# Score products of two tiles per TensorE run, value products of a batch in one run: attention ahead of a dense layer, fp32, one core

## The chip, the core and the metric

The kernel runs on one core of one Trainium2 chip. The time is the device time of one execution in microseconds (us). Before the change the median of three runs is 931.36 us (931.02 to 931.78); one execution was recorded by the hardware profiler, with a span of 929.1 us at the full granted TensorE clock (1.000).

Engines are named as the profile names them: PE is TensorE's matmul, PEld its weight load, DVE VectorE, ACT ScalarE, POOL GpSimd, SP the engine that issues most transfers. `L258` is line 258 of the kernel before.

## The reference, cut to what matters

All in fp32. Batch 8, 8 heads, 576 tokens, head width 64. Keys and values are averaged over groups of 8 tokens, so 72 keys are left per head.

```python
k_p = k.reshape(B, H, Sp, pool, D).mean(axis=3)          # 576 tokens -> 72 keys
v_p = v.reshape(B, H, Sp, pool, D).mean(axis=3)
scores = scale * np.matmul(q, k_p.transpose(0, 1, 3, 2))
scores = scores - np.max(scores, axis=-1, keepdims=True)
attn = np.exp(scores)
attn = attn / (np.sum(attn, axis=-1, keepdims=True) + 1e-09)
attn_out = np.matmul(attn, v_p)
x = attn_out.transpose(0, 2, 1, 3).reshape(B * S, H * D)  # 4608 x 512
h = x @ w_in                                              # 512 -> 2048
s = np.sin(alpha * h)
g = h + s * s / (alpha + 1e-09)
out = g @ w_out                                           # 2048 -> 512
```

## The kernel before

**Two stages.** Up to about 530 us the kernel computes attention and `g` together: while TensorE does the first dense layer for one block of 512 tokens (`u`, nine of them), the attention of a later batch is woven in. After that comes the second dense layer (L963), which the change does not touch.

**Slots.** The first dense layer uses a fast scheme with seven products in place of eight. A block `u` has 28 slots, four groups `J` of seven (`k` = 0 to 6). Each slot ends with one product: four matmuls of 256 columns, which the profile records as eight (L666). What follows from the product of slot `k` on ScalarE and VectorE (`left0` to `left6`) is issued at the start of the next slot, ahead of the attention work of that slot. Every engine runs its instructions in the order in which they are written here.

```python
def left0(): b6 = bank(); scalar.copy(b6, b1)                 # L692; then squares of the group before (L679)
def left1(): finish(Q)                                        # VectorE, L733: two adds for the group before
def left2(): store_g(Q); b7 = bank(); scalar.copy(b7, b6)     # L704
             scalar.copy(p5, b5)                              # L706
def left3(): sin(b1); square                                  # ScalarE, L672, L679
def left4(): add(g[1,:,1], b7, p5)                            # VectorE, L645
def left5(): add(g[0,:,1], b6, p5); sin(g[1,:,1])             # VectorE L645, ScalarE L672
             add(g[0,:,0], b1, s)                             # VectorE, L645
def left6(): sin(g[0,:,1]); [square]; sin(b7)                 # ScalarE
# ...
p = (1, 5, 6, 2, 7, 3, 4)[k]     # products of the slots; 1 and 5 start b1 and b5,
                                 # 6 adds into b6, 2 into b1, 7 into b7, 3 into b6, 4 into b7
product(p, ...)                  # L666
```

So product 6 waits for the copy L692, product 7 for the copy L704, and product 4 (slot k = 6) for the add of `left4`, which reads b7 first. There are eight PSUM banks of 512 fp32 columns: five turn for the dense layer (four per group), and three (5, 6, 7) serve the attention (`abank`).

**Scores.** A batch has 576 tokens: four tiles of 128 and one of 64 rows. A score tile is 16 matmuls of 64 x 64 (64 x 32 for the last tile), 72 columns each, recorded as 32 (L258); heads of one half (`e`) share a bank.

```python
def products(i):
    ps = [self.abank([P, NP, Sp]) for e in range(2)]
    for hp in range(NP):
        for r, q in columns(hp, i):
            for e in range(2):
                s = slice(64 * e, 64 * e + 64)
                k = kb[s, hp, :] if b else self.kb2[s, 2 * hp + e, :]
                nc.tensor.matmul(ps[e][r:r + q.shape[-1], hp, :], q[s], k, start=True, stop=True)
    return ps
def shift(i, e, ps):
    # n rows: 128, or 64 for the last tile
    nc.vector.tensor_reduce(out=mx[:n], in_=ps[:n], axis=AX, op=OP.max)                      # L265
    nc.vector.tensor_tensor(out=ex[...], in0=ps[:n], in1=mx..., op=OP.subtract)              # L266
def score(i):
    for e, ps in enumerate(products(i)):
        shift(i, e, ps)
def exp(i):    # ScalarE, L275: one activation over the tile's 8 heads x 72
def norm(i):   # VectorE: sum over the keys (L287), reciprocal (L279); GpSimd: product (L280)
def turn(i):   # VectorE: 32 x 32 transposes of ex into tr (L404, L405)
def move(part):
    for a in (2 * part, 2 * part + 1):
        for s in range(2):
            for c in range(2):
                nc.sync.dma_start(out=..., in_=...)      # tr to aM, L416: 16 transfers per batch
```

The tile `tr` is one buffer; `turn_q` (L194) writes it again for the next queries, after the moves have landed.

**Values.** The main run (slot 25) holds 512 tokens of each head pair in four banks; the 64 tokens left follow one slot later in two banks. In both, 64 of the 72 keys come first (64 x 64 tiles) and the last 8 keys after them (32 x 128 tiles).

```python
def values(hps, banks):
    for o, (main, _) in zip(ps, parts):
        for e, (w, x) in enumerate(main):
            nc.tensor.matmul(o[64 * e:64 * e + 64], w, x, start=True, ...)                   # L456
    for o, (_, (w, x)) in zip(ps, parts):
        nc.tensor.matmul(o, w..., x, start=False, stop=True, ...)                            # L458
    for hp, o in zip(hps, ps):
        to_x(...)                                                                            # ScalarE, L431
def values_rest(banks):
    ps = [self.psum([P, 2, 64], i) for i in banks]
    # the same in two steps, L478 and L481, and to_x
```

**The schedule** of attention work by slot, for the first block and for the steady ones:

```python
# u == 0 (batch 1):
    for i in range(5):
        at((4, 5, 6, 7, 8)[i], A.q_t, i)
        at((7, 8, 9, 11, 12)[i], A.score, i)
        at((9, 9, 14, 14, 15)[i], A.exp, i)
        at((10, 10, 15, 15, 16)[i], A.norm, i)
        at((13, 13, 16, 17, 17)[i], A.turn, i)
    at(10, self.combine_w_in, 2, (0, 1, 2, 3), self.nc.gpsimd)
    at(10, self.combine_w_in, 3, (0, 1, 2, 3), self.nc.gpsimd)
    at(17, A.move, 0); at(17, A.move, 1)
    # ...
# 0 < u < last (batches 2 to 7):
    for i in range(5):
        at((1, 3, 4, 5, 6)[i], A.score, i)
        at((8, 9, 10, 10, 10)[i], A.exp, i)
        at((9, 10, 11, 11, 12)[i], A.norm, i)
        at((12, 12, 13, 14, 14)[i], A.turn, i)
    at(14, A.move, 0); at(14, A.move, 1)
    # turn_q in slots 22 to 25
    at(25, lambda: A.values((0, 2, 1, 3), A.free_banks()))
    at(26, lambda: A.values_rest((5, (self.turn + 1) % 5)))
    at(26, self.att[b + 1].k_t)                          # L228: keys of the next batch
```

Of the kernel before, what the change touches and what calls it, by code (L numbers as in the profile page):

```python
# [13 lines left out]
F32 = mybir.dt.float32  # L14
AX = mybir.AxisListType.X
AF = mybir.ActivationFunctionType
OP = mybir.AluOpType
PSUM = bass.MemoryType.PSUM

P = 128  # L20
# [20 lines left out]
class Kernel:  # L41
# [171 lines left out]
    def attention(self, b):  # L213
# [2 lines left out]
        kb, ex = self.kblk[b % 2], self.ex  # L216
        rows = (P, P, P, P, 64)
        scale = 1.0 / (D ** 0.5) / POOL
        row = lambda i: 5 if b == 0 else i
        E = lambda n, i, h0, h1: ex[:n, row(i), h0:h1, 0:Sp]  # L220
        aT = []

        def k_t():
# [18 lines left out]
        def columns(hp, i):  # L242
# [4 lines left out]
                return [(64 * c, self.qt[b][:, i, hp, 2 * c:2 * c + 2].rearrange("p t i -> p (t i)")) for c in range(2)]  # L247
            return [(32 * a, self.qt[b][:, a, hp, 4]) for a in range(2)]

        def products(i):  # L250

            ps = [self.abank([P, NP, Sp]) for e in range(2)]
            for hp in range(NP):
                for r, q in columns(hp, i):
                    for e in range(2):
                        s = slice(64 * e, 64 * e + 64)
                        k = kb[s, hp, :] if b else self.kb2[s, 2 * hp + e, :]
                        nc.tensor.matmul(ps[e][r:r + q.shape[-1], hp, :], q[s], k, start=True, stop=True)  # L258
            return ps

        def shift(i, e, ps):

            n = rows[i]
            mx = self.sm.tile([P, NP], F32, name="mx")
            nc.vector.tensor_reduce(out=mx[:n], in_=ps[:n], axis=AX, op=OP.max)  # L265
            nc.vector.tensor_tensor(out=ex[:n, row(i), e::2, 0:Sp] if b == 0 else ex[:n, i, 4 * e:4 * e + 4, 0:Sp], in0=ps[:n],  # L266
                                    in1=mx[:n].unsqueeze(2).to_broadcast([n, NP, Sp]), op=OP.subtract)

        def score(i):
# [1 line left out]
                shift(i, e, ps)  # L271

        def exp(i):
            e = E(rows[i], i, 0, H)
            nc.scalar.activation(out=e, in_=e, func=AF.Exp, scale=scale)  # L275

        def divide(i, sm, eng):
            n = rows[i]
            nc.vector.reciprocal(out=sm[:n], in_=sm[:n])  # L279
            eng.tensor_tensor(out=E(n, i, 0, H), in0=E(n, i, 0, H),  # L280
                              in1=sm[:n].unsqueeze(2).to_broadcast([n, H, Sp]), op=OP.mult)

        def norm(i):

            n = rows[i]
            sm = self.sm.tile([P, H], F32, name="sm")
            nc.vector.tensor_reduce(out=sm[:n], in_=ex[:n, i, :, 0:Sp + 1], axis=AX, op=OP.add)  # L287
            divide(i, sm, nc.gpsimd)

        def new_a():  # L290
            self.aM = self.ap.tile([P, 4, 5, 5, 32], F32, name="aM")

        def k_head(hp):

# [24 lines left out]
        def products_head(hp):  # L319
# [3 lines left out]
            for e in range(2):  # L323
                for tp in range(2):
                    q = self.qt_tiles(b)[:, hp, 2 * e + tp, :]
                    for r in (0, 64):
                        for u in range(2):
                            s = slice(64 * u, 64 * u + 64)
                            nc.tensor.matmul(ps[r:r + 64, u, 2 * e + tp, :], q[s, r:r + 64], self.kb2[s, 2 * hp + e, :], start=True, stop=True)

        exs = ex[:].rearrange("p i h c -> p (i h) c")

        def soft_head(hp):

# [34 lines left out]

        def a0_views():  # L370

            x = self.aM[:].rearrange("p a h t i -> p (a h t i)")[:, 0:5 * S].rearrange("p (h n) -> p h n", h=5)
            return x[:, 0:4], x[:, 4]

        def a_head(g, banks):
# [20 lines left out]
            nc.scalar.copy(out=self.last_t[:], in_=ps)  # L396

        def turn(i):
            n = rows[i]
            if i == 0:  # L400
                self.tr = self.new_tr()
            tr = self.tr[:n].rearrange("p (c s h t i) -> p c s h t i", c=2, s=2, h=5, i=32)[:, :, :, :, i, :]
            x = ex[:n, i].rearrange("p (s h) k -> p s h k", s=2)
            nc.vector.transpose(out=tr[:, :, :, 0:4].rearrange("p c s h i -> p s h c i"), in_=x[..., 0:64].rearrange("p s h (c i) -> p s h c i", c=2))  # L404
            nc.vector.transpose(out=tr[:, :, :, 4].rearrange("p c s (h k) -> p c s h k", h=4),  # L405
                                in_=x[..., 64:Sp].unsqueeze(1).to_broadcast([n, 2, 2, 4, Sp - 64]))

        def move(part):

            tr = self.tr.rearrange("p (c s h t i) -> p c s h t i", c=2, s=2, h=5, i=32)  # L410
            for a in (2 * part, 2 * part + 1):
                flat = lambda x: x.rearrange("p h t i -> p h (t i)")[:, :, 0:160 if a < 2 else 128]
                for s in range(2):
                    for c in range(2):
                        r = 64 * s + 32 * c
                        nc.sync.dma_start(out=flat(self.aM[r:r + 32, a]), in_=flat(tr[32 * a:32 * a + 32, c, s]))  # L416

        def to_x(ps, hp, t0, m):

# [14 lines left out]
        def value_parts(hp, rest):  # L434

            vm, vz = self.vp[b]
            g, s = divmod(hp, 2) if b == 0 else (hp % 2, hp // 2)
            if b == 0:
                aM, aR = (self.last_t[:, 0:4], self.last_t[:, 4]) if rest else a0_views()
                w = slice(0, 64) if rest else slice(0, 4 * P)  # L440
                r = 32 * hp
                return ([(vm[64 * s:64 * s + 64, 2 * g + e], aM[64 * s:64 * s + 64, 2 * g + e, w]) for e in range(2)],
                        (vz[r:r + 32, 0:2], aR[r:r + 32, w]))
            order = lambda x: x.rearrange("p a t i -> p t a i") if b == 1 else x.rearrange("p a t i -> p a (t i)")
            at = lambda r, n, h: self.aM[r:r + n, 0:2, h, 4, :] if rest else order(self.aM[r:r + n, :, h, 0:4, :])
            r = 64 * s + (0 if rest else 32 * g)
            return ([(vm[64 * s:64 * s + 64, 2 * g + e], at(64 * s, 64, 2 * g + e)) for e in range(2)],
                    (vz[r:r + 32, 2 * g:2 * g + 2], at(r, 32, 4)))

# [9 lines left out]
            for hp, o in zip(hps, ps):  # L459
                to_x(o.rearrange("p (t j) -> p j t", t=4), hp, 0, 512)  # L460

        def free_banks():

            return 5, 6, 7, (self.turn + 4) % 5

        def values_rest(banks):

            order = (0, 1, 2, 3) if b == 0 else (0, 2, 1, 3)
            parts = {hp: value_parts(hp, True) for hp in order}
            if b == 0:  # L470
                ps = [self.psum([P, 64], i) for i in banks]
                at = dict(zip(order, ps))
            else:
                ps = [self.psum([P, 2, 64], i) for i in banks]
                at = {hp: ps[hp // 2][:, hp % 2] for hp in order}
            for j, hp in enumerate(order):
                for e, (w, x) in enumerate(parts[hp][0]):
                    nc.tensor.matmul(at[hp][64 * e:64 * e + 64], w, x, start=(b == 0 or j < 2), stop=False, skip_group_check=True)  # L478
            for hp in order:
                w, x = parts[hp][1]  # L480
                nc.tensor.matmul(at[hp], w.rearrange("p e d -> p (e d)"), x, start=False, stop=True, skip_group_check=True)  # L481
            self.vp.pop(b)
            for i, x in enumerate(ps):
                to_x(x, i if b == 0 else slice(2 * i, 2 * i + 2), 512, 64)

        return SimpleNamespace(**{f.__name__: f for f in (k_t, q_t, products, score, exp, norm, new_a, turn, move, values, values_rest, free_banks,
                                                          k_head, q_head, rest_q, products_head, soft_head, norm_head, norm_rest, a_head, a_rest)})


# [325 lines left out]
    def carry(self, u):  # L815
# [5 lines left out]
        if u == 0:  # L821
# [15 lines left out]
            at(7, self.load_v, 1, 1)  # L837
            for i in range(5):
                at((4, 5, 6, 7, 8)[i], A.q_t, i)
                at((7, 8, 9, 11, 12)[i], A.score, i)  # L840
                at((9, 9, 14, 14, 15)[i], A.exp, i)
                at((10, 10, 15, 15, 16)[i], A.norm, i)
                at((13, 13, 16, 17, 17)[i], A.turn, i)
            at(10, self.combine_w_in, 2, (0, 1, 2, 3), self.nc.gpsimd)
            at(10, self.combine_w_in, 3, (0, 1, 2, 3), self.nc.gpsimd)
            at(15, A0.exp, 4)
            at(20, A0.norm_rest)
            at(23, A0.a_rest)
# [1 line left out]
            at(17, A.new_a)  # L850
            at(17, A.move, 0)
            at(17, A.move, 1)
            at(25, lambda: A.values((0, 2, 1, 3), A.free_banks()))
            at(26, lambda: A.values_rest((5, (self.turn + 1) % 5)))
            at(9, self.load_q, 2)
            at(14, self.load_q, 3)
            for e in range(2):
# [5 lines left out]
            at(0, self.sums_of_x, u, 3)  # L863
        if 0 < u < last:
            A = self.att[b]
            for i in range(5):
                at((1, 3, 4, 5, 6)[i], A.score, i)
                at((8, 9, 10, 10, 10)[i], A.exp, i)
                at((9, 10, 11, 11, 12)[i], A.norm, i)
                at((12, 12, 13, 14, 14)[i], A.turn, i)  # L870
            at(14, A.new_a)
            at(14, A.move, 0)
            at(14, A.move, 1)
            for i in range(2):
                at((0, 1)[i], self.load_v, b, i)
                if b < last:
                    at(12, self.load_k, b + 1, i)
            at(25, lambda: A.values((0, 2, 1, 3), A.free_banks()))
            at(26, lambda: A.values_rest((5, (self.turn + 1) % 5)))
            if b < last:  # L880
                at(26, self.att[b + 1].k_t)
            if u + 3 <= last:
# [324 lines left out]
```

## Time and profile before

| | |
|---|---|
| time | 931.36 us (931.02 to 931.78) |
| span in the profile | 929.1 us |
| granted TensorE clock | 1.000 |
| period of a steady batch (one `u`) | 57.35 us |
| in one such period (151.20 to 208.55): PE, PEld busy | 57.35, 46.50 us |
| DVE, ACT, POOL busy in it | 38.89, 39.60, 19.66 us |
| first block (35.50 to 94.00): PE, DVE, ACT, POOL busy | 55.50, 41.49, 44.21, 35.63 us of 58.50 |

The busy time of PE counts a matmul until its result is out, and matmuls overlap, so PE looks busy also where the starts are further apart than they need be. The starts say more: two L666 records in a row start 0.216 us apart.

An answer of the profile is read like this. In the chain, each row is a start in us, a duration in us, and what ran: engine, tile, line, how often. In the timeline, a bracket at the end of a row gives the idle time of the engine ahead of it and the instruction that ended it.

### The profile page before, as it was taken

The page shows a single profiled execution, that of the slowest core. Times are in us where ns is not written, and L with a number is a line of the kernel's source. Part 1 is how long each engine was busy: PE and PEld are TensorE (multiplying, and loading weights), DVE is VectorE, ACT ScalarE, POOL GpSimd, SP SyncE. Part 2 cuts the span into 40 slices and gives each one's busy share as a digit, 9 for nine tenths or more (in the row PEclk, how much of TensorE's full clock was granted, in tenths as well). Part 3 has the DMA queues.
Part 4 walks back from the last instruction along what each step waited for, and adds up shares of the span by engine and source line. Part 5 has one row for each costly group of instructions (what it writes and reads, how often), then busy time and mean ns, then how long its engine had stood idle before and what let it go on. Part 6 is the DMA issues. An engine that isn't in the chain of part 4 may idle for free.

```text
span 929.1 us, 17658 instructions
## 1 busy us (share of the span) xinstructions
PE 912.3 (98%) x6953; PEld 815.0 (88%) x6953; DVE 687.6 (74%) x1060; ACT 439.8 (47%) x1011; POOL 158.9 (17%) x154
## 2 busy tenths in 40 slices
PE   7999999999999999999999999999999999999997
PEld 6676887878878788787888899999999999999997
DVE  7576776757767576673366889988888888988894
ACT  4686586775857658676786631111111211112111
POOL 4284250522505225050000000000000000000000
PEclk9999999999999999999999999999999999999999
DMA  9975655857567556635626247162536353443501
GB/s 251 241 200 167 183 155 167 241 168 189 158 179 218 172 137 160 181 110 169 256 83 207 91 142 217 40 205 51 175 82 166 90 158 99 138 118 110 147 14 39
DMA packets 141298, 141.12 MB, mean 152 GB/s; under 512 B 49808, under 2 KB 111008, under 8 KB 141216
## 3 DMA queue, kind: packets, MB, share of 16 engines
q1 hardware_dynamic: 140144, 138.81, 51.9%
q10 hardware_dynamic: 1072, 1.19, 0.5%
q8 instruction: 55, 0.90, 0.4%
q14 instruction: 27, 0.22, 0.1%
HBM read 75.37 MB, written 47.19 MB: 132 GB/s over the span
## 4 chain that ended last, share of the span: by engine, by line
PE 93%; ACT 2%; DVE 1%; issue 0%; DMA 0%; POOL 0%; SPq 0%; DVEq 0%; ACTq 0%; POOLq 0%
PE PS L666 45%; PE PS L963 41%; PE PS L258 3%; PE PS L456 2%; PE PS L458 1%; PE PS L481 0%; ACT s L672 0%; PE PS L478 0%; ACT ex L275 0%; PE PS L228 0%; DVE h L733 0%; DVE h L645 0%; ACT s L679 0%; PE PS L239 0%; DMA out_dram<-o 0%
## 5 line engine op out<-in xcount | busy, mean ns | idle before, releaser
L666 PE MATMUL PS<-home,a 128*128 128x256 f32 x1152 | 267.2, 382 | 1.0 <-DVE h L645 1.0
L666 PEld LDWEIGHTS PS<-home,a 128*128 128x128 f32 x1152 | 215.0, 190 | 38.7 <-issue 5.3
L666 PE MATMUL PS<-home,as 128*128 128x256 f32 x864 | 201.1, 382 | 1.2 <-POOL a L537 1.2
L666 PEld LDWEIGHTS PS<-home,as 128*128 128x128 f32 x864 | 161.5, 190 | 25.4 <-POOL a L537 1.6
L963 PE MATMUL PS<-s,wb 128*128 128x144 f32 x896 | 119.3, 286 | 0.4 <-ACT PS L1076 0.4
L963 PEld LDWEIGHTS PS<-s,wb 128*128 128x128 f32 x896 | 113.7, 190 | 0.7 <-ACT PS L1076 0.6
L679 ACT ACTIVATE s<-s,c 128x256 f32<-128x256 f32 (+1 forms) x216 | 110.0, 572 | 0.0
L117 POOL TENSOR_TENSOR kvin<-kvin 96x768 f32<-96x768 f32 (+3 forms) x42 | 69.1, 1646 | 205.3 <-DMA kvin<-in_v_dram 192.5
L645 DVE TENSOR_TENSOR h<-PS,p 128x512 f32<-128x512 f32 x72 | 49.2, 684 | 64.2 <-PE PS L666 33.3
L672 ACT ACTIVATE s<-h,al 128x256 f32<-128x256 f32 x144 | 65.1, 501 | 53.7 <-DVE h L645 53.7
L1076 ACT COPY PS<-PS 128x144 f32<-128x144 f32 x56 | 14.7, 263 | 146.0 <-PE PS L963 144.6
L672 ACT ACTIVATE s<-PS,al 128x256 f32<-128x256 f32 x144 | 60.2, 469 | 37.8 <-DVE h L733 20.1
L963 PE MATMUL PS<-r,wb 128*128 128x144 f32 x512 | 73.2, 286 | 0.0
L963 PE MATMUL PS<-s,a 128*128 128x144 f32 x512 | 73.2, 286 | 0.0
L963 PEld LDWEIGHTS PS<-r,wb 128*128 128x128 f32 x512 | 67.1, 190 | 0.1
L963 PEld LDWEIGHTS PS<-s,a 128*128 128x128 f32 x512 | 67.0, 190 | 0.0
L733 DVE TENSOR_TENSOR h<-PS,s 128x512 f32<-128x512 f32 x36 | 24.7, 685 | 50.8 <-ACT s L679 50.7
L1095 ACT COPY PS<-PS 128x144 f32<-128x144 f32 x56 | 14.7, 263 | 88.2 <-PE PS L963 88.2
L963 PE MATMUL PS<-s,we 128*128 128x144 f32 x384 | 54.9, 286 | 0.0
L963 PE MATMUL PS<-x,wb 128*128 128x144 f32 x384 | 54.9, 286 | 0.0
L963 PEld LDWEIGHTS PS<-s,we 128*128 128x128 f32 x384 | 50.3, 190 | 0.1
L963 PEld LDWEIGHTS PS<-x,wb 128*128 128x128 f32 x384 | 50.3, 190 | 0.0
(170 smaller groups left out, 1208.4 us busy)
## 6 DMA issues: line engine op xcount, KB each, us to landing
g_bridge<-h SPq DMA_DIRECT2D x72, 512.0 KB
r<-g_bridge SPq DMA_DIRECT2D x31, 1152.0 KB
out_dram<-o SPq DMA_DIRECT2D x128, 72.0 KB
kvin<-in_k_dram SPq DMA_DIRECT2D x14, 576.0 KB
q<-in_q_dram SPq DMA_DIRECT2D x7, 1024.0 KB
kvin<-in_v_dram SPq DMA_DIRECT2D x14, 512.0 KB
aM<-tr SPq DMA_DIRECT2D x56, 100.0 KB
aM<-tr SPq DMA_DIRECT2D x56, 80.0 KB
```

The source lines that it names most:

```text
L117: self.nc.gpsimd.tensor_tensor(out=t[..., 0:w] if w > D else out, in0=t[..., 0:w], in1=t[..., w:2 * w], op=OP.add)
L258: nc.tensor.matmul(ps[e][r:r + q.shape[-1], hp, :], q[s], k, start=True, stop=True)
L456: nc.tensor.matmul(o[64 * e:64 * e + 64], w, x, start=True, stop=False, skip_group_check=True)
L458: nc.tensor.matmul(o, w.rearrange("p e d -> p (e d)"), x, start=False, stop=True, skip_group_check=True)
L645: add = lambda o, x, y: nc.vector.tensor_tensor(out=o, in0=x, in1=y, op=OP.add)
L666: nc.tensor.matmul(ps[:, jj, :], self.A[p][:, kk, f * P:(f + 1) * P], x[:, kk, :], start=(start and jj == 0 and kk == 0), stop=(kk == 1), ...
L672: nc.scalar.activation(out=G.s[:, i, jj, j, :], in_=src[:, jj], func=AF.Sin, scale=self.al[:, f:f + 1])
L679: nc.scalar.activation(out=x, in_=x, func=AF.Square, scale=self.c[:, f:f + 1])
L733: add = lambda o, x, y: self.nc.vector.tensor_tensor(out=o, in0=x, in1=y, op=OP.add)
L963: nc.tensor.matmul(out, W[:, J // 2, J % 2, :], A[:, J, :], start=(start and J == 0), stop=(J == self.NJ - 1), skip_group_check=True)
L1076: nc.scalar.copy(out=x1[:, 0, :], in_=x0[:, 1, :])
L1095: nc.scalar.copy(out=x1[:, 1, :], in_=x1[:, 0, :])
```

## The change

Three things are changed in batches 1 to 7; batch 0 keeps its own path.

1. **Scores of two tiles per run.** `two_scores(j)` does the matmuls of tiles `2j` and `2j + 1` in one run, in four banks: 5 and 6 for the first, and for the second bank 7 with the bank of the five that is free at that time. The 64-token tile has no run of its own: its scores go with tile 3, into the free columns of that tile's two banks, as two more head columns (6 in place of 4). Maximum and subtract then take both banks in one instruction, 576 elements a row, or 864 for tile 3. Exponential, sum, reciprocal, product and turn take four tiles in place of five, the last one 12 heads wide. In the second run tile 3 is shifted ahead of tile 2.
2. **Values of all 576 tokens in one run.** `all_values` joins the main products and those of the last 64 tokens, which now share one bank; two copies of one element on VectorE keep products of different row halves in that bank apart. The layout of `aM` and `tr` changes with it: each of the 16 moves is one piece of 736 or 704 elements a row.
3. **Places in the schedule.** Two score runs in slots 3 and 5 (10 and 12 in the first block) in place of five; in the first block exponentials, sums and turns lie in slots 14 to 17, and GpSimd's fourth combination of weights moves from slot 10 to 16.

The purpose is fewer visits of TensorE to its small tiles, each of which costs a change there and back, and fewer instructions on VectorE and ScalarE.

```diff
+        def two_scores(j):
+            x = (self.turn + 1) % 5
+            views = []
+            for i, (c, d) in ((2 * j, (5, 6)), (2 * j + 1, (x, 7))):
+                m = 6 if i == 3 else NP
+                ps = self.PS[:, c:d + 1:d - c, 0:m * Sp].rearrange("p e (h k) -> p e h k", h=m)
+                views.append((i, m, ps))
+                for t in (i, 4) if i == 3 else (i,):
+                    for hp in range(NP):
+                        r0, h = (64 * (hp // 2), NP + hp % 2) if t == 4 else (0, hp)
+                        for r, q in columns(hp, t):
+                            for e in range(2):
+                                s = slice(64 * e, 64 * e + 64)
+                                nc.tensor.matmul(ps[r0 + r:r0 + r + q.shape[-1], e, h, :], q[s], kb[s, hp, :], start=True, stop=True)
+            for i, m, ps in views[::-1 if j else 1]:
+                mx = self.sm.tile([P, 2, 6], F32, name="mx2")
+                nc.vector.tensor_reduce(out=mx[:, :, 0:m], in_=ps, axis=AX, op=OP.max)
+                nc.vector.tensor_tensor(out=E(i).rearrange("p (e h) k -> p e h k", e=2), in0=ps,
+                                        in1=mx[:, :, 0:m].unsqueeze(3).to_broadcast([P, 2, m, Sp]), op=OP.subtract)
 ... (exp, norm: four tiles, tile 3 with 12 heads)
         def turn(i):
+            nc.vector.transpose(out=main..., in_=x[:, :, 0:4, 0:64]...)
+            if i < 3:
+                nc.vector.transpose(out=keys, in_=x[:, :, 0:4, 64:Sp]...)
+            else:
+                for c in range(2):
+                    nc.vector.transpose(out=keys[:, c], in_=x[:, :, 0:4, 64:Sp])
+                nc.vector.transpose(out=tr[..., 640:704]..., in_=x[:, :, 4:6, 0:64]...)
+                for s in range(2):
+                    nc.vector.transpose(out=tr[:, 0, s, 704:736]..., in_=x[:, s, 4:6, 64:Sp]...)
 ... (move: 16 transfers, each 736 or 704 elements a row)
+        def all_values():
+            hps = 0, 2, 1, 3
+            ps = dict(zip(hps, (self.psum([P, 4 * P], i) for i in (5, 6, 7, (self.turn + 4) % 5))))
+            rest = self.psum([P, 4, 64], (self.turn + 1) % 5)
 ...
+            def ordered():
+                nc.vector.tensor_copy(out=self.sm.tile([P, 1], F32, name="order")[:], in_=rest[:, 1, 0:1])
+            halves(ps[2], main[2], True)
+            halves(rest[:, 0], more[0], True)
+            halves(rest[:, 1], more[1], False)
+            ordered()
+            for hp in (0, 1):
+                halves(ps[hp], main[hp], True)
+            halves(rest[:, 2], more[2], False)
+            halves(rest[:, 3], more[3], False)
+            halves(ps[3], main[3], True)
+            for o, hp in ((rest[:, 0], 0), (rest[:, 1], 1)):
+                last_keys(o, more[hp])
+            ordered()
+            for hp in hps:
+                last_keys(ps[hp], main[hp])
+            for hp in (2, 3):
+                last_keys(rest[:, hp], more[hp])
 ... (to_x for the five banks)
 # u == 0
-                at((7, 8, 9, 11, 12)[i], A.score, i)
-                at((9, 9, 14, 14, 15)[i], A.exp, i)
-                at((10, 10, 15, 15, 16)[i], A.norm, i)
-                at((13, 13, 16, 17, 17)[i], A.turn, i)
+            for i in range(2):
+                at((10, 12)[i], A.two_scores, i)
+            for i in range(4):
+                at((14, 15, 15, 15)[i], A.exp, i)
+                at((15, 15, 16, 16)[i], A.norm, i)
+                at((16, 16, 17, 17)[i], A.turn, i)
-            at(10, self.combine_w_in, 3, (0, 1, 2, 3), self.nc.gpsimd)
+            at(16, self.combine_w_in, 3, (0, 1, 2, 3), self.nc.gpsimd)
 # 0 < u < last
-                at((1, 3, 4, 5, 6)[i], A.score, i)
-                at((8, 9, 10, 10, 10)[i], A.exp, i)
-                at((9, 10, 11, 11, 12)[i], A.norm, i)
-                at((12, 12, 13, 14, 14)[i], A.turn, i)
+            for i in range(2):
+                at((3, 5)[i], A.two_scores, i)
+            for i in range(4):
+                at((8, 9, 10, 10)[i], A.exp, i)
+                at((9, 10, 11, 11)[i], A.norm, i)
+                at((12, 12, 13, 13)[i], A.turn, i)
-            at(25, lambda: A.values((0, 2, 1, 3), A.free_banks()))
-            at(26, lambda: A.values_rest((5, (self.turn + 1) % 5)))
+            at(25, A.all_values)
```

## The prediction, made before the changed kernel was run

> **What bounds the kernel now.** I read the page's busy shares first, then the chain that ended last.
>
> ```profile
> PE 912.3 (98%) x6953; PEld 815.0 (88%) x6953; DVE 687.6 (74%) x1060; ACT 439.8 (47%) x1011; POOL 158.9 (17%) x154
> ...
> PE 93%; ACT 2%; DVE 1%; issue 0%; DMA 0%; POOL 0%; SPq 0%; DVEq 0%; ACTq 0%; POOLq 0%
> ```
>
> TensorE is the bound, and only time on its own stream counts. Next comes the chain in order of time for one batch in the steady part (start, duration, what):
>
> ```profile
> 218.07 0.66 PE PS L258 x32
> 218.74 1.92 PE PS L666 x8
> ...
> 225.83 0.64 PE PS L258 x32
> 226.46 33.19 PE PS L666 x152
> 259.65 1.88 PE PS L456 x16
> 261.53 1.07 PE PS L458 x8
> 262.60 1.93 PE PS L666 x8
> 264.53 0.39 PE PS L478 x16
> ```
>
> A slot is eight L666 records. 152 of them take 33.19 us, so a slot alone is 1.73 to 1.75 us; between two score runs it is 1.92. The single starts in the trace say why. L666 starts are 0.216 us apart; the first score starts 0.309 after the last L666; eight groups of four run 0.0625 us apart, the first 0.05 late; then L666 comes back 0.11 late and its second record at 0.320 instead of 0.216. A score run thus holds 0.50 us of work and 0.093 + 0.05 + 0.11 + 0.104 = 0.36 us of switching. The batches repeat every 57.35 us with almost no gap on TensorE.
>
> But the chain in a later batch shows who stands just behind it:
>
> ```profile
> 284.31 8.07 PE PS L666 x37
> 292.38 0.48 ACT PS L704
> 292.87 0.51 ACT p L706
> 293.38 1.74 ACT ex L275 x3
> ...
> 296.13 0.69 DVE h L645
> 296.87 20.99 PE PS L666 x96
> ```
>
> The copy into b7, three exponentials, a row sum and the add of left4 release slot 13 with no time to spare. The timeline of the weight loads shows the same two places one batch earlier, by what ended the idle time in brackets:
>
> ```profile
> 235.07 1.59 PEld L666 LDWEIGHTS PS<-home,a 128*128 128x128 f32 x8 [0.18 <-ACT PS L704]
> ...
> 238.67 3.32 PEld L666 LDWEIGHTS PS<-home,a 128*128 128x128 f32 x16 [0.28 <-DVE h L645]
> ```
>
> So in slots 9 to 13 ScalarE and VectorE have zero slack, although their shares are 47% and 74%.
>
> [...]
>
> **The change part by part.** Scores: five runs per batch become two. Matmuls stay the same in number. TensorE saves 3 x 0.36 = 1.07 us a batch, 7.5 us over seven batches, if nothing else waits.
>
> Values: today the main run takes 3.15 us over its neighbours (262.854 - 259.276 less two L666 pitches), the rest run about 1.14 (L478 0.39, L481 0.59 and L228 0.40 in a batch without a wait, plus the 0.09 ahead of them, less 0.33 that L228 needs alone); together 4.29. One run: both row halves carry 4 x 0.43 + 4 x 0.06 = 1.96 (the spacing of the groups of four in L456 and L478), the last keys 0.21 + 1.04 + 0.21 (two rounds each, 0.105 apart in L481, 0.52 in L458), switches about 0.5: 3.9. It saves 0.4 a batch, 3 us in all. The two waits of L228 for L431 (0.9 us by the waits) also go. The sum on TensorE alone is 7.5 + 3 + 0.9 = 11.4 us: 920.
>
> VectorE's cost falls: maximum and subtract of 288 elements take 0.450 and 0.457 us, of 576 elements 0.741 and 0.758 (L337, L339), so about 1.03 and 1.06 at 864. In pitch: 1.45 for a tile, 2.05 for the 864 one; 6.4 us against 8.6 per batch. But it comes in two lumps, and the second lies badly. I follow one batch with slot 0 at 211.9 as before.
>
> The first run falls in slot 3 at 217.15, after finish (ends 218.28); VectorE does it by 221.3, in time. The second starts in slot 5 at 221.96; its 24 groups end at 223.5. Only then can VectorE begin: tile 3 from 223.8 to 225.8, tile 2 to 227.3, and then the first add of left5, ending 227.97. Before, that add ended at 226.56. ScalarE follows as before: sine (left6) 0.04 after, then sines and squares, 2.3 us from the first sine to the copy b1 to b6 (L692): 230.33, before 230.15. From L692 to the end of L704 it was 230.15 to 235.02 (copy, squares, 1.28 us table load, two exponentials); now 235.2. TensorE arrives 1.07 us early at slot 9, waits there some 0.4 us and at slot 11 the rest: slot 11 starts at 235.4, before 235.13. Two exponentials (0.58 + 0.96), the sum of 12 heads (1.03), reciprocal and left4's add then end at 239.07, before 238.61, so slot 13 starts 0.5 us later than before. The 1.07 us is gone and 0.5 more. My error here is about 0.4 us either way, mostly the unmeasured 864-element forms.
>
> Ordering: in slot 25 the third and fourth rest products wait for a VectorE copy. VectorE is then here:
>
> ```profile
> 256.95 2.37 DVE L194 STREAM_TRANSPOSE tr<-q 128x1024 f32<-128x1024 f32 x2 [4.60 <-DMA aM<-tr]
> ...
> 260.95 0.75 DVE L194 STREAM_TRANSPOSE tr<-q 64x256 f32<-64x256 f32 x2
> ```
>
> It can serve the copy at 261.7. The transfers that free tr cost 0.64 us of issue each whatever their size, 16 before and after; their start moves from 244.6 to about 244.1, so the copy runs near 261.2. TensorE starts the run at 259.58 + 0.5 = 260.07, and its upper row half is free for those products 0.05 + 0.86 later, at 260.98. With the restart behind the copy it loses about 0.5 us, more or less what the merged run saves. A steady batch comes out 0.5 - 0.4 + 0.5 = 0.6 us longer; six of them 3.6 us.
>
> First batch (u = 0): exponentials, sums and turns of all four tiles are pushed into slots 14 to 17. TensorE gains 1.7 us up to slot 13 (five runs of 0.86 or less and a 0.74 us wait for kblk at 44.6, against two runs of 1.4 and 1.6). Exponential 0 still starts at 65.6, for left5's add ends near 61.7 as before (second run at 57.3, then 2.05 + 1.45 + 0.69 on VectorE, with the starting lag). ScalarE then has L692, 1.3 us of squares, and exponential 1, which ends near 68.6. From there VectorE does, in the order of the program: sum 1 (to 69.6), finish (0.6 + 1.2, to 71.5), turns 0 and 1 (0.82 each, to 73.2), sums 2 and 3 (0.86 + 1.19, to 75.3), turn 2 (to 76.1), and turn 3 (about 1.4), which first waits for GpSimd's product of tile 3 (1.15 x 1.5 = 1.7 from 75.3, to 77.0): 78.5. Only then comes left4's add, which slot 20 needs because that slot adds into b7. Before, this add ended at 75.26 and slot 20 began at 75.32; now it ends near 79.2, so slot 20 comes 4 us later. The move to aM starts 4 us later too, so the ordering copy in slot 25 may cost 1 to 2 us more. Less 0.4 and 0.45 from values and L228, I get 4 to 6; I take 2.5, since this is my longest chain of estimates and it assumes that nothing slides into the gaps.
>
> Sum: 931.4 + 3.6 + 2.5 = 937.5; I say 937.
>
> **Rivals.** (a) TensorE stays the only bound and keeps all: 920. For it: 98% busy and four switches less. Against it: the chain at 292 to 297, where ScalarE and VectorE already release TensorE. (b) Half is kept: if the 864-element forms are quicker than I think, or TensorE's wait at slot 9 is hidden, a steady batch is 0.5 us shorter: about 927. (c) The ordering copies become the new wait: each batch loses 1.5 us in slot 25 because L194 sits before the copy in VectorE's queue: 942. (d) The first batch's turns come so late that slot 25 waits for its data: 2 us more.
>
> **Range and chances.** A clean gain is capped at 11 us, 1.2%, so faster by over 2% (below 912.7) has 2%. Over 2% slower (above 950) needs more than 2 us lost in each batch or both (c) and (d): 4%. Within 2%: 94%. The range runs from 924 (b, with a harmless first batch) to 945 (c, with the full loss of the first batch).
>
> **What would show it.** Score runs per batch two instead of five: right for the switches. The batch period against 57.35: 57.9 is my sum, 56.0 is rival (a). In the waits, TensorE or its loads waiting for ACT L692 and L704 in slots 9 and 11 and for DVE L645 in slot 13 would prove the ScalarE and VectorE part; waits in the new value run for a VectorE copy would prove the ordering; a gap of some 4 us before slot 20 of u = 0, released by DVE L645, the first batch. I am wrong if the period shrinks by a microsecond with none of these waits: then VectorE's lump did not delay left5's add, or ScalarE had slack that the timeline hides.

## The result and the profile after

The changed kernel takes 973.79 us (median of 4 runs, 971.06 to 978.79) against 931.19 us for the kernel before: a ratio of 1.0463, 95% interval 1.0414 to 1.0511. The prediction was 937.0 with a range of 924 to 945, so the result lies far above it.

First the page of the kernel after, busy shares and the chain that ended last:

```profile
PE 920.7 (95%) x6953; PEld 828.6 (85%) x6953; DVE 667.7 (69%) x990; ACT 434.4 (45%) x995; POOL 154.1 (16%) x147
...
PE 83%; DVE 7%; ACT 4%; issue 1%; POOL 0%; DMA 0%; SPq 0%; DVEq 0%; ACTq 0%
```

TensorE does the same 6953 matmuls, but its share of the chain fell from 93% to 83%, and VectorE's rose from 1% to 7%, although VectorE has less to do (667.7 us against 687.6). So TensorE waits, and for VectorE. The waits of TensorE in the kernel after (in order: what waits, for what; us in total, times, longest) name the place:

```profile
PE PS L721 <- DVE ex L273: 26.7, 10, 2.9
PE PS L721 <- DVE h L700: 5.9, 7, 4.7
...
PE PS L721 <- ACT PS L759: 2.4, 4, 0.6
```

In the kernel after, L721 is the dense product (L666 before), L269 the score product, L272 and L273 the maximum and the subtract behind it, L700 the adds of left4 and left5 (L645 before), L747 and L759 the copies into b6 and b7 (L692 and L704 before). The second and third line are the waits that the prediction described. The first was in no step of it: ten times, a dense product waits until VectorE has subtracted the maxima of a score run. The timeline shows one of them, in the batch u = 3 (start, duration, what; idle time before and its releaser in brackets):

```profile
231.82 1.23 PE L269 MATMUL PS<-kblk,q 64*64 64x72 f32 x64
...
232.86 0.75 DVE L272 TENSOR_REDUCE mx<-PS 128x8 f32<-128x576 f32 x1
233.65 0.76 DVE L273 TENSOR_TENSOR ex<-PS,mx 128x576 f32<-128x576 f32 x1
...
234.32 0.75 DVE L272 TENSOR_REDUCE mx<-PS 128x8 f32<-128x576 f32 x1
235.10 0.76 DVE L273 TENSOR_TENSOR ex<-PS,mx 128x576 f32<-128x576 f32 x1
235.91 3.72 PE L721 MATMUL PS<-home,a 128*128 128x256 f32 x16 [2.86 <-DVE ex L273]
```

The dense product at 235.91 writes b1, into which no score was written. It neither reads nor overwrites anything of tiles 0 and 1, and still it starts only after both subtracts.

The second thing that the prediction lacked is in the mean clock, 0.987 against 1.000 before. Here are two stretches of the kernel after, one before and one behind such a wait (window; its length, busy time of PE, PEld, DVE, ACT, POOL with instructions; then the granted clock, the DMA share and GB/s):

```profile
290.00:296.80 6.80, 6.80 (x86) 5.82 (x88) 4.58 (x7) 4.92 (x11) 0.00 (x0) 1.00 0.58 133
299.70:303.10 3.40, 3.14 (x8) 2.54 (x9) 0.20 (x1) 0.00 (x0) 1.91 (x1) 0.51 0.90 318
```

In the second one TensorE runs at half clock: dense products start 0.427 us apart in it, and 0.216 us elsewhere. The chain of the same place has the loss in time:

```profile
299.96 5.24 PE PS L721 x16
305.19 1.72 PE PS L269 x94
```

Two slots of dense products take 5.24 us here. In the batch u = 2, which has neither thing, they take 3.65.

The periods, from one value run to the next, for the batches u = 2 to 6: before 57.35, 57.35, 58.20, 57.35, 57.35; after 58.29, 63.95, 65.56, 65.16, 61.16. The first of the latter is the undisturbed one.

### The profile page after: what moved, and what is told of

The parts are those of the page before. It is cut to its first block, busy times and chain, and to the rows that moved or that the text cites. A ratio compares the mean times of both kernels' runs of the same rounds, so it can differ in the third digit from the quotient of the medians.

```text
span 969.3 us, 17586 instructions
## 1 busy us (share of the span) xinstructions
PE 920.7 (95%) x6953; PEld 828.6 (85%) x6953; DVE 667.7 (69%) x990; ACT 434.4 (45%) x995; POOL 154.1 (16%) x147
## 4 chain that ended last, share of the span: by engine, by line
PE 83%; DVE 7%; ACT 4%; issue 1%; POOL 0%; DMA 0%; SPq 0%; DVEq 0%; ACTq 0%
PE PS L1019 39%; PE PS L721 39%; PE PS L513 2%; DVE mx L272 2%; DVE ex L273 2%; ACT s L734 2%; DVE h L788 1%; PE PS L269 1%; PE PS L517 1%; DVE sm L305 1%; DVE h L700 1%; ACT s L727 1%; ACT PS L747 0%; ACT ex L299 0%; ACT p L761 0%
## 5 line engine op out<-in xcount | busy, mean ns | idle before, releaser
L721 PE MATMUL PS<-home,a 128*128 128x256 f32 x1152 | 274.8, 391 | 25.3 <-DVE ex L273 17.1
L721 PEld LDWEIGHTS PS<-home,a 128*128 128x128 f32 x1152 | 222.8, 196 | 62.7 <-DVE ex L273 18.0
L721 PE MATMUL PS<-home,as 128*128 128x256 f32 x864 | 203.2, 384 | 10.5 <-DVE ex L273 9.6
L721 PEld LDWEIGHTS PS<-home,as 128*128 128x128 f32 x864 | 163.4, 191 | 35.8 <-DVE ex L273 10.3
L700 DVE TENSOR_TENSOR h<-PS,p 128x512 f32<-128x512 f32 x72 | 49.2, 684 | 98.2 <-PE PS L721 56.6
L727 ACT ACTIVATE s<-h,al 128x256 f32<-128x256 f32 x144 | 65.2, 501 | 78.1 <-DVE h L700 78.1
L727 ACT ACTIVATE s<-PS,al 128x256 f32<-128x256 f32 x144 | 60.0, 467 | 54.2 <-PE PS L721 42.4
```

The source lines that it names most:

```text
L700: add = lambda o, x, y: nc.vector.tensor_tensor(out=o, in0=x, in1=y, op=OP.add)
L721: nc.tensor.matmul(ps[:, jj, :], self.A[p][:, kk, f * P:(f + 1) * P], x[:, kk, :], start=(start and jj == 0 and kk == 0), stop=(kk == 1), ...
L727: nc.scalar.activation(out=G.s[:, i, jj, j, :], in_=src[:, jj], func=AF.Sin, scale=self.al[:, f:f + 1])
```

## The experiments

Theory A: tiles 1 and 3 are read by VectorE as one view with a stride over two banks, x and 7, where x is (turn + 1) mod 5. The ordering of accesses treats this view as all banks from x to 7, so that a product into a bank between them is made to wait for the read. Of the four banks that a group of slots draws, b1 is x + 1 and b6 is x + 2 (mod 5). The dense product behind the first score run goes to b1, the one behind the second to b6. So both wait for x = 0, 1, 2, only the first for x = 3, none for x = 4. A batch draws 16 banks, so x grows by one from batch to batch (from u = 0 to u = 1 by two, since the score runs of u = 0 lie one group of slots later): 1, 3, 4, 0, 1, 2, 3. That gives 2, 1, 0, 2, 2, 2, 1 waits for u = 0 to 6: ten, and just in the batches in which the trace has them. Rival B: VectorE's lump is too long wherever it lies, and TensorE would wait for it with any view.

**own_banks**: tiles 1 and 3 are shifted one bank at a time; products, slots and everything else stay.

```diff
-            for i, m, ps in views[::-1 if j else 1]:
-                mx = ...
-                nc.vector.tensor_reduce(out=mx[:, :, 0:m], in_=ps, ...)
-                nc.vector.tensor_tensor(out=..., in0=ps, ...)
+            for v in views[::-1 if j else 1]:
+                shift_two(*v)
+        def shift_two(i, m, ps):
+            ...
+            for e in ((0, 1) if i % 2 else (slice(0, 2),)):
+                nc.vector.tensor_reduce(out=mx[:, e, 0:m], in_=ps[:, e], ...)
+                nc.vector.tensor_tensor(out=out[:, e], in0=ps[:, e], ...)
```

> The changed kernel, with one edit: tiles 1 and 3, whose two banks (x and 7) are not neighbours, are shifted bank by bank (two maxima and two subtracts in place of one each). Theory A (false wait): the one VectorE read over banks x and 7 is ordered as if it read all banks from x to 7, so the next dense product, whose bank lies between, waits until VectorE is done. Then the ten gaps of 2.5 to 3.1 us behind score runs vanish, no half-clock windows are left in the steady batches, a steady batch takes 58.3 to 58.6 us, and the time is 939 to 948. Rival B: the dense product really needs what VectorE does in that time, or VectorE is simply too busy: gaps stay, 968 or more.

Measured: 942.34 us (941.71 to 945.37), ratio 1.0129 (1.0109 to 1.0150), 31.5 us less than the kernel after. VectorE does more instructions than after, and yet all ten waits are gone. Timeline of own_banks, the same place of u = 3 (L278 and L279 are maximum and subtract there, L727 the dense product):

```profile
224.30 1.23 PE L269 MATMUL PS<-kblk,q 64*64 64x72 f32 x64
...
225.34 0.75 DVE L278 TENSOR_REDUCE mx<-PS 128x8 f32<-128x576 f32 x1
225.47 3.72 PE L727 MATMUL PS<-home,a 128*128 128x256 f32 x16
```

The dense product follows the scores at once, while VectorE has only begun. Waits of own_banks:

```profile
PE PS L727 <- DVE h L706: 5.8, 7, 4.7
PE PS L727 <- ACT PS L753: 5.4, 7, 2.5
PE PS L727 <- ACT PS L765: 4.2, 7, 0.6
```

All three kinds are predicted ones: slots 13 and 20 (left4's add), slot 9 and slot 11 (the two copies). The two for the copies are longer in sum than in the kernel after, where the ten waits took their place in most batches. The balance: 26.7 us of waits removed; half-clock time removed, 10.2 - 1.2 = 9.0 (the starts of matmuls beyond their usual distance, added up in the half-clock stretches of either trace; the mean granted clock is 0.987 after and 0.998 in own_banks); waits that come back, (5.4 + 4.2) - (0.9 + 2.4) = 6.3. That leaves 29.4. These figures come from the two profiled executions, whose spans differ by 969.3 - 939.9 = 29.4 as well, closer than the sums are accurate; the medians differ by 31.5.

**phase**: the kernel after, its turn through the five banks begun one bank later. Then the gaps must sit in other batches. (With this start, one bank that the first batch uses by its number comes up in the turn too, so part of what that batch computes differs; the trace is read for the places of the gaps alone.)

```diff
-                self.bt, self.left, self.group, self.turn = {}, [], None, 2
+                self.bt, self.left, self.group, self.turn = {}, [], None, 3
```

> The changed kernel, with the turn of the five dense banks started one bank later (3 in place of 2), so that x is one higher in every block; no work differs. Theory A: the gaps move with x. First block (x = 2) both score runs, u = 1 (x = 4) none, u = 2, 3 and 4 (x = 0, 1, 2) both, u = 5 (x = 3) only the first, u = 6 (x = 4) none: nine gaps, 965 to 980 us. Rival B: the pattern stays as it is (u = 2 alone free of gaps, u = 1 and 6 with one).

Measured, one run: 970.15 us. By the batches u = 0 to 6 there are 2, 0, 2, 2, 2, 1, 0 waits, which is the arithmetic above with x one larger: u = 1, which had one wait, has none, and u = 2, which had none, has two. The line of the waits:

```profile
PE PS L721 <- DVE ex L273: 24.5, 9, 3.4
```

Same work, same schedule, other bank numbers, and the waits move with the numbers. With own_banks this settles A against B.

**held**: own_banks, and tile 2 is shifted only behind left5 (slot 6; in the first block slot 13), so that left5's first add stands behind tile 3 alone.

```diff
+            if j:
+                shift_two(*views[1])
+                held.append(views[0])
 ...
+            at(6, A.shift_held)        # steady batches; at(13, ...) in the first block
```

> As own_banks, and the shift of tile 2 is issued after left5 (slot 6, slot 13 in the first block) in place of ahead of it. Theory C (the prediction's second part): VectorE's lump of tiles 3 and 2 delays left5's first add by 1.4 us and with it L692 and L704 of the next group; then the waits of slots 9 and 11 shrink and a steady batch is 0.7 to 1.1 us shorter than in own_banks, 4 to 7 us in all. Rival: ScalarE alone holds slots 9 to 13, and nothing changes by more than 1 us.

Measured: 932.31 us, ratio 1.0011 (0.9995 to 1.0026), 10.0 us less than own_banks, where 4 to 7 had been expected. The period fell from 58.41 to 56.95, by 1.46 where 0.7 to 1.1 had been expected, and the value run of the first block starts 1.9 us sooner (89.62 against 91.54). Waits of held:

```profile
PE PS L736 <- DVE h L715: 5.8, 7, 4.7
...
PE PS L736 <- ACT PS L762: 1.0, 1, 1.0
...
PE PS L736 <- ACT PS L774: 0.6, 1, 0.6
```

The waits for the copies into b6 (L762) and b7 (L774) are left in the first block only. So in the steady batches it was the lump of slot 5, through left5's add, that held ScalarE back, as the prediction had it. I had undersized what this costs.

**two_runs**: own_banks, with the value products in two runs again (slots 25 and 26), in the new layout, without ordering copies.

```diff
-            at(25, A.all_values)
+            at(25, A.main_values)
+            at(26, A.two_rest)
```

> As own_banks, with the value products in two runs as in the kernel before (512 tokens in slot 25, the last 64 in slot 26, two banks, no ordering copies). By the prediction's TensorE working the one run saves 0.4 us a batch and the ordering takes 0.5 back: within 2 us of own_banks. If the ordering copies were a large cost (rival c of the prediction) this is 5 us or more faster than own_banks; if they cost nothing, 3 us slower.

Measured: 940.89 us (940.24 to 942.12) beside 942.34. The single value run brings nothing; if anything it costs. The starts say how much on TensorE: from the start of the value run to the first dense product behind the next batch's key transposes it takes 6.16 us in two runs (before and two_runs alike, in a batch without a wait there), 6.44 in one (own_banks, held, early). But here a later wait could absorb the difference, so it is taken up again below.

**norm_late, first_block, both**: held, with the two waits that it still has taken on. norm_late puts the sum of tile 3's twelve heads one slot later, behind left4's add; first_block spreads the first block's softmax; both has the two edits.

```diff
 # norm_late, steady batches
-                at((9, 10, 11, 11)[i], A.norm, i)
-                at((12, 12, 13, 13)[i], A.turn, i)
+                at((9, 10, 11, 12)[i], A.norm, i)
+                at((12, 12, 13, 14)[i], A.turn, i)
 # first_block, u == 0; the moves in slot 19 in place of 17
-                at((14, 15, 15, 15)[i], A.exp, i)
-                at((15, 15, 16, 16)[i], A.norm, i)
-                at((16, 16, 17, 17)[i], A.turn, i)
+                at((12, 12, 15, 15)[i], A.exp, i)
+                at((13, 13, 16, 16)[i], A.norm, i)
+                at((15, 15, 17, 19)[i], A.turn, i)
```

> The held kernel, with the 12-head sum of tile 3 in slot 12 and its turn in slot 14 in the steady batches, so that left4's add no longer stands behind that sum. My theory (the remaining 0.57 us wait at slot 13 is left4's add queued behind the 1.06 us sum of tile 3): the wait at slot 13 goes, periods about 56.5 instead of 56.95, six batches give 2.7 us: 929.6 against held's 932.3. Rival (the wait at slot 13 is the late exponential on ScalarE, not the queue on VectorE): periods stay 56.9 to 57.0, 932.

> The held kernel, with the first block's exponentials spread over slots 12, 12, 15, 15, sums 13, 13, 16, 16, turns 15, 15, 17, 19 and the moves in slot 19. My theory (slot 20 waits 5.1 us because left4's add stands behind four sums and four turns that all lie in slots 14 to 17): that wait goes to under 1 us, but the moves start later and the value run of that block waits for their landing by 1 to 2 us: 927.5 to 929.5 against held's 932.3. Rival (VectorE is simply full there, whatever the order, or the whole wait moves into the value run): 931 to 934.

> The two edits of the other runs together. If they are independent as my theory has it: about 925 (ratio 0.993 to the kernel before). Rival: one of them only moves the wait, 928 to 932.

Measured: norm_late 931.20 us, ratio 0.9988 (0.9973 to 1.0003): the waits at slot 13 are gone and the periods are 56.5 to 56.9, but with five periods 1.7 us shorter together than in held the gain is smaller than the 2.7 expected. first_block 928.84, ratio 0.9978 (0.9967 to 0.9989): the 5.1 us gap at slot 20 is gone. New in its place are a wait of 1.4 us in slot 24, where TensorE waits for a VectorE product of the first batch's 64-token tile that stands behind the last turn, and one start in the value run that comes 0.92 us after the one before it, where 0.42 is usual. The chain of first_block shows where the latter comes from (L456 the moves, L194 the turns of q, L534 the ordering copy, L528 the value products):

```profile
87.79 0.58 SPq L456
88.41 2.10 DMA aM<-tr
90.53 1.81 DVE tr L194 x2
...
92.82 0.72 DVE tr L194 x2
93.54 0.05 DVE order L534
...
93.64 1.31 PE PS L528 x12
```

The move ends late, the turns of q that reuse tr start late, and the ordering copy queues behind them: rival (c) of the prediction, though it costs 0.5 us here. both comes to 927.51 us, ratio 0.9959 (0.9938 to 0.9980). The single gains over held, 1.1 and 3.5 us, add up to 927.7: the two waits are independent. The 925 I had hoped for is not reached because norm_late gave less.

**early**: own_banks and norm_late's order, with the score runs of the steady batches in slots 1 and 3 and nothing held back. The first run borrows the bank in which b7 is built two slots later, and what this kernel computes is wrong; its time alone is read.

```diff
-            x = (self.turn + 1) % 5
+            x = (self.turn + (1 if j or b == 1 else 2)) % 5
-                at((3, 5)[i], A.two_scores, i)
+                at((1, 3)[i], A.two_scores, i)
```

> Score runs of tiles shifted bank by bank, with both score runs of a steady batch two slots earlier (slots 1 and 3) and no holding back of tile 2, with tile 3's sum in slot 12 and its turn in slot 14. My theory (the second lump in slot 5 delays left5's add, and through it ScalarE's chain to slots 9, 11 and 13): early lumps are done before left5's add, the waits at slots 9, 11 and 13 go, periods 56.3 to 56.7; with the first block unchanged (5.1 us wait at slot 20) 928 to 931. Rival (VectorE's or ScalarE's total is what counts, not the place): periods 57.5 to 58.4, 937 to 942.

Measured: 930.81 us, ratio 0.9991 (0.9976 to 1.0006), periods 56.38 to 56.41 but for one of 57.02. With the first block unchanged, the gain in the steady batches comes from the place of the lump alone: VectorE does all its work, early enough.

**both_two, beside both_again**: both, with the value products in two runs (the edit of two_runs). In this schedule no later wait is left to absorb a gain.

> The kernel with both schedule edits, but with the value products in two runs and without the ordering copies. In the kernels with one value run TensorE takes 6.44 us from the start of the value run to the first dense product behind the key transposes of the next batch, in those with two runs 6.16. Theory (the one run and its ordering copies cost 0.28 us a batch, and nothing waits later in the batch any more that would absorb it): periods 56.2 us, six batches give 1.7 us: about 926 against 927.5 beside it. Rival (a later wait absorbs it, as it seemed to when tried with the waits of slots 9 to 13 still there): no difference, within 0.5 us.

> The kernel with both schedule edits and one value run, beside the one with two, on the same chip: 927.5 again, periods 56.5.

Measured: both_two 923.77 us (923.08 to 924.46), ratio 0.9909 (0.9884 to 0.9933); both_again 926.97 (926.25 to 927.65), ratio 0.9943 (0.9921 to 0.9966). Two of the five periods are 56.21, and the shortest two of both_again 56.49: the single value run with its ordering copies costs 0.28 us in a batch (how much of it is the copies, and how much the order of the products, was not taken apart). Two more are 56.70, because there TensorE waits some 0.5 us at the key transposes (L233) for the copy that frees their bank, a wait that the single run did remove. One of both_again is 57.46, because in u = 3 the ordering copy stands behind the turn of q, and the value run is 0.97 us longer:

```profile
258.82 0.75 DVE L194 STREAM_TRANSPOSE tr<-q 64x256 f32<-64x256 f32 x2
...
259.51 0.11 DVE L534 COPY order<-PS 128x1 f32<-128x1 f32 x1
259.67 0.43 PEld L528 LDWEIGHTS PS<-aM,vm 64*64 64x64 f32 x12 [0.46 <-DVE order L534]
```

The sum of the five is 1.1 us less than in both_again (283.10 against 284.16). The first block gives more, 1.8 us up to the value run of u = 1 (142.36 against 144.17). There the value run of both_again waits 1.1 us for the moves and then 0.5 us for the ordering copy, and starts at 86.04; that of both_two starts at 84.96, before the last move has landed. both_two is the best kernel of the study, 0.9% faster than the kernel before: the merged scores without the strided view and without the merged values, with the places of held, norm_late and first_block.

## Why the prediction was wrong, point by point

**TensorE saves 3 x 0.36 us a batch, if nothing else waits.** This is the step that failed, in its condition: ten dense products waited, 26.7 us in all, for VectorE to have read tiles 1 and 3 from the strided view. The size of the saving was right. From the last dense start before a score run to the first one behind it, less the usual 0.216, the five visits of before take 4 x 0.754 + 0.728 = 3.74 us, the two of after 1.254 + 1.691 = 2.95; with the late second record of three visits fewer (3 x 0.104) that is 1.11 us a batch. But the change also altered how VectorE reads the scores, and I asked of that read only what it costs VectorE, and not which TensorE writes it would be ordered against. I looked for waits in the work that depends on the scores; this one holds work that doesn't. Of the 42.6 us that were lost, own_banks got 31.5 back by splitting this view alone: the waits and the half-clock time that follows from them. That the wait follows bank numbers is shown; whether it could be seen from the edit alone is another matter: the index with the step d - c over banks x and 7 was in the diff, with banks of the dense products lying between.

**Clock.** I had taken 1.000 for granted. The 10.2 us at half clock came on top of the waits, and follow from them: in own_banks (mean granted clock 0.998), without the ten waits, one stretch is left (at 79.2 us, behind the gap of slot 20), and in phase (0.985) one begins at 185.2, in the batch u = 2, which has neither a wait nor a stretch in the kernel after.

**Slots 9, 11 and 13.** Right, to a tenth. The batch u = 2 of the kernel after has no disturbance; its timeline:

```profile
187.48 1.99 PE L721 MATMUL PS<-home,as 128*128 128x256 f32 x8 [0.24 <-ACT PS L747]
...
191.80 1.99 PE L721 MATMUL PS<-home,a 128*128 128x256 f32 x8 [0.59 <-ACT PS L759]
...
195.71 3.72 PE L721 MATMUL PS<-home,a 128*128 128x256 f32 x16 [0.19 <-DVE h L700]
```

Counted from the start of the second score run (178.47), left5's first add ends at 6.02 us (predicted 227.97 - 221.96 = 6.01), the copy into b7 at 13.28 (13.24), left4's add at 17.19 (17.11). held then showed that the lump was the cause.

**Values.** The single run was to save 0.4 us and the ordering copy to take 0.5 back; on TensorE it came out 0.28 us longer (0.40 in the batch u = 2 of after) instead of 0.1. So the term had the right sign and was mis-sized by 0.2 to 0.3 us, and the waits of L228 (0.9 us in all) did go, but they are two, and the longer run is paid in every batch. Together with slot 13 this gives the 58.29 us of the undisturbed batch, against 57.9 in the prediction. Rival (c), 1.5 us per batch, did not come in this size. In most steady batches the ordering copy waited only for the products. In u = 3 it stood behind the turn of q in every kernel with one value run, as (c) has it, for 0.06 us (own_banks) to 0.97 (both_again).

**First block.** The chain was right: slot 20 waits for left4's add behind the four sums and turns (longest wait 4.7 us, gap 5.1; predicted about 4). The chain of the kernel after:

```profile
80.75 1.64 POOL ex L307
...
83.89 0.58 DVE h L700
...
84.52 7.13 PE PS L721 x24
```

It ends in GpSimd's product of tile 3, the turn and then the add, as worked out. What failed was the discount from "4 to 6" to 2.5 "since this is my longest chain of estimates". In own_banks the value run of u = 1 starts 5.81 us later than before (150.69 against 144.88), less 1.06 for the batch u = 1 (if it lost what the others lost): 4.8. Of this 1.2 is the half-clock stretch behind the gap, which was no part of my sum; so 3.6 is left, nearer to 4 than to 2.5.

**What the sum was worth without the missed step.** own_banks is 11.0 us slower than before (942.34 against 931.35), 3.6 + 2.5 = 6.1 was predicted. So the steps that I saw were 5 us short (1.2 of it the clock), within the range, and the one that I did not see was six times as large. The rivals named waits that replace the removed ones, but all of them for data or for the ordering copy, and so the range had no room for it.

## What to carry to other kernels

When an edit turns several accesses into one larger or strided one, ask what lies between its ends: the program may order everything in that span against it, and the victim is then work that shares no data with it (here ten dense products, 26.7 us). A sign in the profile is a wait whose releaser neither made the operands of the waiting instruction nor used its destination. Split such a view into pieces that hold only what is read, even at the price of more instructions (here 31.5 us less); and place a lump of a secondary engine so that the operation the bottleneck needs next does not stand behind it (10.0 us between own_banks and held).

Switches that were merged away were worth only their own cost (1.1 us of 57 in a batch for three), and one merged run with an engine's copies in the middle cost more than two without (0.28 us a batch).

## What the runs showed of the hardware that was not expected

Short waits of TensorE cost more than their length here: the two slots behind the gap that ended at 299.96 us took 5.24 us, where an undisturbed batch has 3.65. The granted clock fell to half for 3.4 us (once 6.8) at 64.1, 84.6, 245.0, 299.7, 309.9 and 364.5 us in the kernel after, each time within 6 us after the start of a gap of 2.5 to 5.1 us (from the start of one matmul to the start of the next). In the same trace gaps of 2.6 to 3.1 us at 52.4, 113.4, 232.8, 373.4 and 427.5 were not followed by one.

The trace gives each of these stretches a length of 3.413 us or twice that, and they start whole multiples of that length apart (from 245.0 to 299.7 it is 16 of them, from there to 309.9 three, from there to 364.5 again 16). So I cut the trace into pieces of 3.413 us, counted from these starts. Here are three pieces with a gap in them and the piece behind each (busy time of PE, then the granted clock):

```profile
241.62:245.04 3.41, 1.38 (x6) 1.00 0.71 192
245.04:248.45 3.41, 3.41 (x9) 0.50 0.59 173
...
361.09:364.50 3.41, 1.48 (x66) 1.00 0.96 223
364.50:367.92 3.41, 2.49 (x6) 0.50 1.04 302
...
111.92:115.33 3.41, 1.67 (x67) 1.00 1.06 217
115.33:118.74 3.41, 2.29 (x11) 1.00 0.93 316
```

The six pieces just ahead of half clock in the kernel after have PE busy for 0.09 to 1.48 us; no other piece at full clock between 30 and 530 us of this trace has less than 1.67. A gap of 2.5 us that lies mostly in one piece was followed by half clock, a gap of 3.1 us that was divided between two was not. In phase the two kinds are apart in the same way (at most 1.14 us and at least 1.92). One gap does not fit: in both and first_block, one of 1.6 us (a wait of 1.4 us) was followed by half clock though PE was busy for 2.00 us of its piece (mean granted clock 0.997 in either profile). This is read from the traces; no run was made to test it, and what decides whether the clock falls was not shown.
